# A linear-attention and token-mixing block: kv products by four token tiles, one low part behind `ol`, one high part on VectorE

## The chip, the core and the metric

The kernel runs on one NeuronCore of a Trainium2 chip. The metric is device time in microseconds for one execution, the median of the runs shown. The profile is one further execution with the hardware profiler on.

## What is computed

`x` is 2048 tokens by 512 channels. Two residual stages follow each other:

```
h  = x + A(layernorm(x))      # linear attention, 32 heads of 16
h2 = h + B(layernorm(h))      # MLP across the 2048 tokens, F = 1792

A: q, k, v = split(x @ wqkv);  pq = q @ w_phi (per head), pk = k @ w_phi
   phi = concat(softmax(p), softmax(-p))            # for q and for k
   kv  = sum over tokens of phi_k^T v;  z = sum over tokens of phi_k
   o   = (phi_q kv) / (phi_q z + 1e-6);  A = o @ wo
B: h = layernorm again; u = gelu(h^T @ w1 + b1); y = u @ w2 + b2, transposed back
```

All in float32. A large product is made as three products of a high part and a low part of each operand (`mm3`: high by high, high by low, low by high); a high part is a rounded copy and a low part is what the copy left.

## The kernel before

**Tiles.** Tokens go by 16 tiles of 128 (`NT`), called t below; channels by four blocks of 128.

**Prelude (lines 217 to 356).** `wqkv` arrives as twelve row blocks. Blocks 4 to 7 belong to k: each is centred (`center`), multiplied with the block-diagonal `w_phi` on TensorE (`fold`) and split into a high part (`hi_w`, ScalarE, or VectorE with `True`) and a low part (`lo_w`, VectorE). The order on TensorE, VectorE, ScalarE and GpSimd is written out by hand up to line 350. `proj(0, ..., True)` makes the first k product by parts: all high weights first (eight products), the low weights last (four).

**k/v stage (lines 358 to 415).** For each t: `k_logits` (TensorE product `pk_ps`, VectorE maximum, minimum and two subtractions, ScalarE exponential), `k_norm` (VectorE sums `sk`, GpSimd multiplies `pk`, and adds it to `zacc`), `v_proj` (TensorE `pv`, ScalarE scales into `vs`), and at six of the tiles the product, logits, exponential and sums of a q tile (`pu`, `eq`, `smq`). `v_kv` runs `kv` for the last two tiles after each second v: 16 products per tile, each with 32 columns of `vs` as weights and 64 columns of `pk`, all added up in one PSUM tile `kvp`. The order of this stage on each engine is made by a planner that simulates the program, so an edit here can move anything in the stage.

**From line 417 the order is by hand.** The last k and v products, then `zB` (line 484: `zacc` summed over tokens on TensorE), which GpSimd needs for every `s_ez` (`ez`, the products of phi_q with z); `s_den` sums `ez` on VectorE and makes the weights `w`, and `s_pq` multiplies `eq` by `w` on GpSimd.

**Attention loop (lines 660 to 701).** 18 iterations `it`; different tiles stand at different steps. In iteration `it`, TensorE does `pn` (phi_q kv of tile it-1, line 547), the transposes `tr` of tile it (line 529), a first piece of other work (half a q product, later a row block of w1), `po` (the product with `wo` of tile it-1, lines 62 to 64, twelve products) and then the rest of the other work (`turn`). On the other engines: ScalarE makes `oh` (high part of `pn`), copies `tr`, and before that takes the moments of the last h (`s_moments`); VectorE makes `ol` (low part of `pn`), sums `smq`, `s_den`, and `h` (the residual, line 572, which reads `po`); GpSimd makes `s_pq`, one reciprocal root, `s_ez` and the low part of `hs`. `pn` and `po` share one PSUM tile: `po` cannot start before `ol` has read `pn`, and the next `pn` cannot start before `h` has read `po`.

The row blocks of w1 come by DMA (`stream`): each has a high part on ScalarE (`his`) and a low part `wlo` on VectorE, made by `flush` at the end of each iteration:

```
    run(ql[:2] + ol + ql[2:] + sm if ql else sm[:1] + ol + sm[1:])
    ...
    if 0 <= it - 1 < NT:
        s_h(it - 1)
    flush()
```

**After the loop** come the rest of the first MLP product, gelu, and the second MLP product (`py`, line 795) with its own split of w2.

Of the kernel before, what the change touches and what calls it, by code (L numbers as in the profile page):

```python
# [9 lines left out]
F32 = mybir.dt.float32  # L10
# [7 lines left out]
P = 128  # L18
S, D, H, DH, F = 2048, 512, 32, 16, 1792
NT = S // P  # L20
KD = D // P
NF = F // P
NG = 8
NPR = 2 * NG
Q_AT = (4, 6, 8, 9, 11, 13)
V_NOT = (0, 1, 11)
Q_TURNS = ((0, 1), (0, 1), (0, 1), (0, 1), (0,), (1,), (0,), (1,))
LAG = 3
WARM = 9
# [4 lines left out]
def block_kernel(ctx: ExitStack, tc: tile.TileContext, x, xT, wT, phic, wo, w1, b1, w2, b2,  # L34
# [34 lines left out]
    wqp = aq.enter_context(tc.tile_pool(name="wqp", bufs=1, side="right"))  # L69
# [1 line left out]
    wql = wqp.tile([P, KD, D], F32R, name="wql")  # L71
    kvB = wqp.tile([P, 2, P], F32, name="kvB")
    kvS = wqp.tile([P, 4, 64], F32, name="kvS")
    sums = wqp.tile([P, NT, NPR, 2, 2], F32, name="smq")
    wqp.tile([P, 504], F32, name="pad")
    wk = aq.enter_context(tc.tile_pool(name="wk", bufs=4, side="right"))

# [7 lines left out]
    kk = a1.enter_context(tc.tile_pool(name="kk", bufs=2))  # L85
# [9 lines left out]
    X, XH, EQ, PK, VS, SQ, PS, W = {}, {}, {}, {}, {}, {}, {}, {}  # L95
# [10 lines left out]
    def split_x(t, raw):  # L106
        X[t] = big.tile([P, 2, KD, P], F32R, name="xs", tag="big")
        split(X[t][:, 0], X[t][:, 1], raw, nc.gpsimd)
# [25 lines left out]
    def signs(e):  # L134
        return e.rearrange("p g (a c h d) -> p (g a) c h d", a=2, c=2, h=2)
# [19 lines left out]
    def negate():  # L155

        if MN:
            ev, mx, mn = MN.pop(0)
            nc.gpsimd.tensor_sub(mn, mn, mx)
            nc.gpsimd.tensor_sub(ev[:, :, 1], mn.unsqueeze(3).to_broadcast([P, NPR, 2, DH]), ev[:, :, 0])  # L160

    def turns(*lists):

        return [ops[i] for i in range(max(map(len, lists))) for ops in lists if i < len(ops)]

    def run(*lists):
        for op in turns(*lists):
            op()

    def exps(t, e):  # L170
        nc.scalar.activation(e, e, AF.Exp, scale=r1[:, t:t + 1])
# [2 lines left out]
        return e.rearrange("p g (a d) -> p (g a) d", d=DH)  # L174

    def k_ops(t, o):
        PK[t] = kk.tile([P, NG, P], F32, name="pk", bufs=len(V_NOT) + 3)
        run(logit_ops(o, PK[t], False))

    def k_logits(t):  # L180
# [1 line left out]
        exps(t, PK[t])  # L182

    def v_out(t, o):
        VS[t] = kk.tile([P, D], F32, name="vs", bufs=4)
        nc.scalar.activation(VS[t], o, AF.Copy, scale=r1[:, t:t + 1])

    def v_proj(t):
        v_out(t, proj(t, wvh, wvl, ps_v, "pv"))
# [11 lines left out]
    def kv(t):  # L201

        for n in range(4):
            for c in range(4):
                g = n // 2 * 4 + c
                j = 2 * g + n % 2
                nc.tensor.matmul(kvp[32 * c:32 * c + 32, n, :], VS[t][:, 32 * j:32 * j + 32],  # L207
                                 PK[t][:, g, n % 2 * 64:n % 2 * 64 + 64], start=(t == 0 and n == 0),
                                 stop=(t == NT - 1), skip_group_check=True)

    def q_sum(t):

        SQ[t] = sums[:, t]
        e = signs(EQ[t])
        return [lambda c=c: nc.vector.reduce_sum(SQ[t][:, :, 1 - c], e[:, :, c], axis=AX.X) for c in range(2)]

    with tc.tile_pool(name="prep", bufs=1) as prep:
# [54 lines left out]
        def parts(c):  # L272
            return [w[:, :, c % 4 * P:(c % 4 + 1) * P] for w in HL[c // 4]]

        def hi_w(c, vector=False):
            if vector:
                nc.vector.tensor_copy(parts(c)[0], FO[c])
            else:
                nc.scalar.activation(parts(c)[0], FO[c], AF.Copy)

        def lo_w(c):
            hi, lo = parts(c)
            nc.vector.tensor_sub(lo, FO[c], hi)
# [4 lines left out]
        with tc.manual_schedule(engines={ET.PE, ET.DVE, ET.Activation, ET.Pool}):  # L288

            nc.gpsimd.tensor_mul(ph.rearrange("p c (a f) -> p c a f", f=DH),  # L290
                                 pc[:, 0:64].rearrange("p (c f) -> p c f", f=DH).unsqueeze(2).to_broadcast([P, 4, 8, DH]),
                                 pc[:, 64:72].unsqueeze(1).unsqueeze(3).to_broadcast([P, 4, 8, DH]))
            center(4, True)
            center(5, False)
            fold(4, ps_q, "pu")
            center(6, True)
            fold(5, ps_q, "pu")
            center(7, False)
            fold(6, ps_v, "pv")
            fold(7, ps_v, "pv")  # L300
            hi_w(4, True)
            hi_w(5, True)
            hi_w(6)
            split_x(0, xr[0])
            hi_w(7)
            for c in range(4, 8):
                lo_w(c)
            split_x(1, xr[1])
            k0 = proj(0, wkh, wkl, ps_k, "pk_ps", True)
            center(8, True)  # L310
            for c in range(9, 12):
                center(c, False)
            k1 = proj(1, wkh, wkl, ps_k, "pk_ps")
            for c in range(8, 12):
                fold(c, *((ps_q, "pu"), (ps_v, "pv"))[c // 10])
            k_ops(0, k0)
            split_x(2, xr[2])
            k_ops(1, k1)
            stats_x(0)
            k2 = proj(2, wkh, wkl, ps_k, "pk_ps")  # L320
            for c in range(8, 12):
                hi_w(c)
            for c in range(8, 12):
                lo_w(c)
            stats_x(1)
            exps(0, PK[0])
            split_x(3, xr[3])
            split_x(4, xr[4])
            v0 = proj(0, wvh, wvl, ps_v, "pv")
            k_ops(2, k2)  # L330
            stats_x(2)
            k3 = proj(3, wkh, wkl, ps_k, "pk_ps")
            k_norm(0)
            center(0, True)
            v_out(0, v0)
            exps(1, PK[1])
            center(1, False)
            exps(2, PK[2])
            v1 = proj(1, wvh, wvl, ps_v, "pv")
            k_ops(3, k3)  # L340
            fold(0, ps_q, "pu")
            fold(1, ps_q, "pu")
            k_norm(1)
            center(2, False)
            v_out(1, v1)
            hi_w(0)
            hi_w(1)
            lo_w(0)
            lo_w(1)
            center(3, False)  # L350
# [35 lines left out]
    def v_kv():  # L386

        nonlocal v
        v_proj(v)
        if v % 2 == 0:  # L390
            kv(v - 2)
            kv(v - 1)
        v += 1

    v = 2
    load_h(4)
    stats_x(4)
    for t in range(3, NT - 1):
# [3 lines left out]
        if t > 3:  # L402
            k_logits(t)
        if t > 3 and t not in V_NOT:
            v_kv()
# [93 lines left out]
    run(q_logits(0))  # L499
    assert v == NT  # L500
    q_mm()
    kv(NT - 2)
    kv(NT - 1)
    run(s_den(2, ps_d, "dn"))
    nc.vector.tensor_mul(kvS, kvp, mask.unsqueeze(1).to_broadcast([P, 4, 64]))

# [88 lines left out]
    COMING, LATER = [], []  # L595

    def his():
        while COMING:
            LATER.append(COMING.pop(0))
            _, raw, wh_ = LATER[-1]  # L600
            nc.scalar.activation(wh_, raw, AF.Copy)  # L601

    def flush():
        his()
        while LATER:
            wl_, raw, wh_ = LATER.pop(0)
            LO.append(nc.vector.tensor_sub(wl_, raw, wh_).ins)  # L607

# [40 lines left out]
    def turn(it):  # L649

        halves = Q_TURNS[it] if it < len(Q_TURNS) else ()
        n = [FN[0] <= it - LAG and FN[0] < NT, min(2, max(0, it - LAG + 1 - FN[1])) if q["logits"] == NT else 0]
        for p in range(2):
            ahead = n[p] + 1 + p + 2 * (it == NT)
            if it >= (LAG - 1, len(Q_TURNS) - 1)[p] and FL[p] < min(NT, FN[p] + ahead):
                fill_load(p)
# [3 lines left out]
    for it in range(NT + 2):  # L660
        if it < NT:
            s_x(it)
        shifted = q["logits"] - len(MN)
        ql = q_logits(0)
        work = turn(it)
        if it > NT:
            his()
        if 0 <= it - 2 < NT:
            s_moments(it - 2)
        if 0 <= it - 1 < NT:  # L670
            s_num(it - 1)
        if it < NT:
            s_tr(it)
        if it + 1 < NT:
            s_pq(it + 1)
        for w in work[:1]:
            w()
        if it == 0:
            s_kv()
        if q["exp"] < shifted:  # L680
            q_exp(0)
        if 0 <= it - 2 < NT:
            s_rstd(it - 2)
        if it + 3 < NT:
            s_ez(it + 3)
        if 0 <= it - 2 < NT:
            s_hn(it - 2)
        negate()
        his()
        sm = q_sums(0) if it == 0 or q["sum"] <= it + 2 else []  # L690
        ol = s_ol(it - 1) if 0 <= it - 1 < NT else []
        run(ql[:2] + ol + ql[2:] + sm if ql else sm[:1] + ol + sm[1:])
        if it > 0 and it + 2 < NT:
            run(s_den(it + 2, ps_t, "tr"))
        if 0 <= it - 1 < NT:
            s_wo(it - 1)
        for w in work[1:]:
            w()
        if 0 <= it - 1 < NT:
            s_h(it - 1)  # L700
        flush()
    flush()
    ms.close()
    a2.close()
# [101 lines left out]
    for n, (sp, p) in enumerate(STEPS):  # L806
        t = 2 * sp
# [93 lines left out]
```

## Time and profile before

| | us |
|---|---|
| median of 3 runs | 528.13 (528.08 to 528.7) |
| the profiled execution, whole | 528.31 |
| its span, first to last instruction | 526.5 |
| TensorE busy | 518.9 |
| VectorE busy | 386.2 |
| ScalarE busy | 278.2 |
| GpSimd busy | 229.1 |
| granted TensorE clock, mean | 0.998 |

A matmul's record overlaps the next one, so the distance between the starts of two records is what a product takes of TensorE's time, not the length of the record. In a row of a timeline stand the start in microseconds from the start of the span, the time, the engine, the line, the operation, output and inputs with their shapes, the count of records, and in brackets the idle time of the engine just before with what ended it. In a row of the chain stand the start, the time and the work. Each kv product and each small float32 product leaves two records.

### The profile page before, as it was taken

How to read it: one execution, taken by the hardware profiler on the slowest of the kernel's cores; microseconds unless marked ns; L12 is line 12 of the kernel's file. 1: busy time of each engine (PE TensorE's matmuls, PEld its weight loads, DVE VectorE, ACT ScalarE, POOL GpSimd, SP SyncE). 2: the span in 40 equal slices, each digit the busy share in tenths (PEclk: the TensorE clock that was granted, in tenths of full speed). 3: DMA queues.
4: the chain of work that ended last, by engine and by line, in shares of the span. 5: the costliest groups of instructions: out<-in, count | busy, mean ns of one | idle time of the engine just before them, and what ended most of it. 6: DMA issues, size and time to landing. Idle time of an engine off the chain costs nothing.

```text
span 526.5 us, 10155 instructions
## 1 busy us (share of the span) xinstructions
PE 518.9 (99%) x4000; PEld 446.6 (85%) x4000; DVE 386.2 (73%) x680; ACT 278.2 (53%) x476; POOL 229.1 (44%) x174
## 2 busy tenths in 40 slices
PE   8999999999999999999999999999999999999996
PEld 7788888887877777787788888888899999999996
DVE  6993999986897899887335425826668878887784
ACT  6998834525267878677657423526444243343330
POOL 2589699876999999884224000000001101101110
PEclk9999999999999999999999999999999999999999
DMA  8644210012303233333245433532015566535631
GB/s 307 203 122 120 83 40 21 1 40 103 99 25 101 101 97 109 114 103 122 81 142 178 119 91 92 169 112 81 20 41 112 146 144 151 128 123 121 161 67 54
DMA packets 45487, 55.85 MB, mean 106 GB/s; under 512 B 3968, under 2 KB 33024, under 8 KB 45440
## 3 DMA queue, kind: packets, MB, share of 16 engines
q1 hardware_dynamic: 43136, 51.38, 30.9%
q0 software_dynamic: 2016, 3.67, 5.3%
q8 instruction: 31, 0.51, 0.4%
q10 hardware_dynamic: 288, 0.17, 0.1%
q14 instruction: 16, 0.13, 0.1%
HBM read 46.81 MB, written 8.39 MB: 105 GB/s over the span
## 4 chain that ended last, share of the span: by engine, by line
PE 95%; DVE 3%; ACT 1%; issue 0%; DVEq 0%
PE py L795 26%; PE pu L62 13%; PE pu L63 12%; PE pu L64 12%; PE pv L63 3%; PE pv L64 3%; PE po L62 3%; PE pv L62 3%; PE po L64 3%; PE po L63 3%; PE pk_ps L62 2%; PE pk_ps L64 2%; PE pk_ps L63 2%; PE pn L547 2%; PE tr L529 2%; PE kvp L207 2%
## 5 line engine op out<-in xcount | busy, mean ns | idle before, releaser
L833 POOL DMA_DIRECT2D out<-ot x14 | 12.4, 998 | 211.4 <-DVE ot L831 211.4
L795 PE MATMUL py<-uf,whi 128*128 128x256 f32 x560 | 96.2, 283 | 0.0
L57 ACT ACTIVATE whi<-wraw 128x1792 fp32r<-128x1792 f32 x28 | 47.7, 1704 | 77.9 <-PE py L795 70.5
L62 PE MATMUL pu<-hs,whi 128*128 128x512 f32 x224 | 87.7, 394 | 0.0
L63 PE MATMUL pu<-hs,whi 128*128 128x512 f32 x224 | 87.2, 389 | 0.0
L64 PE MATMUL pu<-hs,wlo 128*128 128x512 f32 x224 | 86.7, 389 | 0.0
L795 PEld LDWEIGHTS py<-uf,whi 128*128 128x128 f32 x560 | 83.3, 192 | 0.0
L607 DVE TENSOR_TENSOR wlo<-wraw,whi 128x512 fp32r<-128x512 f32 x56 | 48.5, 872 | 44.6 <-ACT whi L601 44.4
L795 PE MATMUL py<-uf,wlo 128*128 128x256 f32 x280 | 69.9, 283 | 0.0
L58 DVE TENSOR_TENSOR wlo<-wraw,whi 128x1792 fp32r<-128x1792 f32 x28 | 56.6, 2022 | 16.7 <-ACT whi L57 16.6
L601 ACT ACTIVATE whi<-wraw 128x512 fp32r<-128x512 f32 x56 | 34.6, 625 | 45.0 <-PE pu L63 40.8
L62 PEld LDWEIGHTS pu<-hs,whi 128*128 128x128 f32 x224 | 42.0, 188 | 9.2 <-ACT hj L579 0.2
L795 PEld LDWEIGHTS py<-uf,wlo 128*128 128x128 f32 x280 | 49.7, 192 | 0.0
L64 PEld LDWEIGHTS pu<-hs,wlo 128*128 128x128 f32 x224 | 42.1, 188 | 8.9
L63 PEld LDWEIGHTS pu<-hs,whi 128*128 128x128 f32 x224 | 42.0, 188 | 8.3
L441 POOL TENSOR_TENSOR ez<-eq,zB 128x1024 f32<-128x1024 f32 x16 | 38.5, 2407 | 3.9 <-ACT zB L485 3.9
L795 PE MATMUL py<-un,whi 128*128 128x256 f32 x224 | 38.4, 283 | 0.0
L195 POOL TENSOR_TENSOR pk<-pk,sk 128x1024 f32<-128x1024 f32 x16 | 31.0, 1939 | 9.9 <-DVE sk L194 7.4
L795 PEld LDWEIGHTS py<-un,whi 128*128 128x128 f32 x224 | 33.2, 192 | 0.1
L465 POOL TENSOR_TENSOR eq<-eq,w 128x1024 f32<-128x1024 f32 x16 | 32.9, 2055 | 0.8 <-DVE w L462 0.8
L199 POOL TENSOR_TENSOR zacc<-zacc,pk 128x1024 f32<-128x1024 f32 x13 | 31.2, 2402 | 0.5
L58 POOL TENSOR_TENSOR hs<-hn,hs 128x512 fp32r<-128x512 f32 x16 | 20.7, 1293 | 17.9 <-ACT hs L57 17.9
(171 smaller groups left out, 1173.4 us busy)
## 6 DMA issues: line engine op xcount, KB each, us to landing
wraw<-in_w SPq DMA_DIRECT2D x112, 256.0 KB, 2.9
xraw<-in_xT SPq DMA_DIRECT2D x16, 256.0 KB, 3.0
xh<-in_x SPq DMA_DIRECT2D x16, 256.0 KB, 2.6
h<-in_x SPq DMA_DIRECT2D x16, 256.0 KB, 2.6
out<-h SPq DMA_DIRECT2D x16, 256.0 KB, 2.0
out<-ot POOLq DMA_DIRECT2D x14, 256.0 KB, 4.7
wraw<-in_wT SPq DMA_DIRECT2D x12, 256.0 KB, 5.2
wo<-in_wo SPq DMA_DIRECT2D x4, 256.0 KB, 4.0
```

The source lines that it names most:

```text
L57: nc.scalar.activation(hi, src, AF.Copy)
L58: lo_engine.tensor_sub(lo, src, hi)
L62: nc.tensor.matmul(o, ah, bh, start=first, stop=False)
L63: nc.tensor.matmul(o, ah, bl, start=False, stop=False)
L64: nc.tensor.matmul(o, al, bh, start=False, stop=last)
L195: nc.gpsimd.tensor_mul(heads(PK[t]), heads(PK[t]), sk.unsqueeze(2).to_broadcast([P, 2 * H, DH]))
L199: nc.gpsimd.tensor_add(zacc, zacc, PK[t])
L441: nc.gpsimd.tensor_mul(EZ[t], EQ[t], zB)
L465: nc.gpsimd.tensor_mul(heads(EQ[t]), heads(EQ[t]), W[t].rearrange("p g c h -> p (g c h)").unsqueeze(2).to_broadcast([P, 2 * H, DH]))
L601: nc.scalar.activation(wh_, raw, AF.Copy)
L607: LO.append(nc.vector.tensor_sub(wl_, raw, wh_).ins)
L795: nc.tensor.matmul(o, a[x], b[:, y], start=start and i == 0, stop=stop and i == 2, skip_group_check=True)
```

## The change

Three edits and the room that they need:

- `kv` is called for four tiles after each fourth v, not for two after each second. The tiles `pk` and `vs` have more buffers for it (8 for 6, and 5 for 4), and the q sums share 8 slots in place of 16.
- In the attention loop the last `flush` of an iteration makes at most one low part. One that is left over is made in the next iteration, behind `ol` and ahead of the sums.
- In the prelude the high part of k's third block (`hi_w(6)`) is made on VectorE in place of ScalarE.

```
+SUMS = 8
-    sums = wqp.tile([P, NT, NPR, 2, 2], F32, name="smq")
+    sums = wqp.tile([P, SUMS, NPR, 2, 2], F32, name="smq")
-        PK[t] = kk.tile([P, NG, P], F32, name="pk", bufs=len(V_NOT) + 3)
+        PK[t] = kk.tile([P, NG, P], F32, name="pk", bufs=len(V_NOT) + 5)
-        VS[t] = kk.tile([P, D], F32, name="vs", bufs=4)
+        VS[t] = kk.tile([P, D], F32, name="vs", bufs=5)
-        SQ[t] = sums[:, t]
+        SQ[t] = sums[:, t % SUMS]
...
-            hi_w(6)
+            hi_w(6, True)
...
-        if v % 2 == 0:
-            kv(v - 2)
-            kv(v - 1)
+        if v % 4 == 0:
+            for t in range(v - 4, v):
+                kv(t)
...
-    kv(NT - 2)
-    kv(NT - 1)
+    for t in range(NT - 4, NT):
+        kv(t)
...
-    def flush():
-        his()
-        while LATER:
+    def flush(n=None):
+        if n is None:
+            his()
+        for _ in range(len(LATER) if n is None else min(n, len(LATER))):
             wl_, raw, wh_ = LATER.pop(0)
             LO.append(nc.vector.tensor_sub(wl_, raw, wh_).ins)
...
+        left = len(LATER)
         his()
         sm = q_sums(0) if it == 0 or q["sum"] <= it + 2 else []
         ol = s_ol(it - 1) if 0 <= it - 1 < NT else []
-        run(ql[:2] + ol + ql[2:] + sm if ql else sm[:1] + ol + sm[1:])
+        run(ql[:2] + ol + ql[2:] if ql else sm[:1] + ol)
+        flush(left)
+        run(sm if ql else sm[1:])
...
-        flush()
+        flush(1)
```

In the built program the kv products stand in five blocks on TensorE where they stood in nine: of 1, 63, 64, 64 and 64 products, in place of 14 and 18 (a fold of four products between them) and seven times 32. In the attention loop one `wlo` moves in three places, from the end of iterations 8, 10 and 12 to behind `ol` of iterations 9, 11 and 13; nothing else in the loop changes its place. In the k/v stage the planner's order of k, v and q products differs from before on all engines.

## The prediction

> **What bounds the kernel now.** I read the chain that ended last first, then TensorE's own waits, then the timelines around each place that the change touches.
>
> ```profile
> PE 95%; DVE 3%; ACT 1%; issue 0%; DVEq 0%
> ```
> ```profile
> core 0 of [0], span 526.5 us
> PE pk_ps L287 <- DVE eps L53: 1.1, 1, 1.1
> PE po L62 <- DVE ol L556: 1.0, 1, 1.0
> PE pk_ps L124 <- ACT wkh L279: 0.8, 1, 0.8
> PE pn L547 <- DVE h L572: 0.2, 1, 0.2
> ```
>
> 95% of the chain is TensorE, and in 526.5 us TensorE waits four times for another engine, 3.1 us in all. So time is saved by work or switching taken off TensorE, or by one of these waits; the change is lost where it makes a new wait. Edit one is of the first kind, edit two aims at the 1.0 (ol), edit three at the 0.8 (wkh). About 0.2% (1.06 us) is what a measurement of this kernel can tell from no change.
>
> **Edit one: kv by four tiles.** It removes no product: 256 kv products stay. What goes is the passage into and out of a block. TensorE's timeline at one block:
>
> ```profile
> 85.33 0.39 PE L63 MATMUL pv<-wvl,xs 128*128 128x512 f32 x1
> 85.56 0.39 PE L64 MATMUL pv<-wvh,xs 128*128 128x512 f32 x1
> 85.88 1.10 PE L207 MATMUL kvp<-pk,vs 128*32 128x64 f32 x64
> 86.91 0.50 PE L62 MATMUL pk_ps<-wkh,xs 128*128 128x512 f32 x1
> 87.24 0.40 PE L63 MATMUL pk_ps<-wkl,xs 128*128 128x512 f32 x1
> ```
>
> Large products start every 0.23 (85.33, 85.56). Into the block the distance is 0.32, out of it 0.33 (86.91 to 87.24): 0.09 + 0.10 = 0.19 lost outside. Inside, the chain has blocks of three lengths:
>
> ```profile
> 36.45 0.57 PE kvp L207 x28
> ...
> 38.10 0.68 PE kvp L207 x36
> ...
> 53.52 1.03 PE kvp L207 x64
> ...
> 141.65 1.03 PE kvp L207 x64
> ```
>
> From 28 to 36 records 0.11, so 0.0138 a record; 64 records are 0.88 of the 1.03, and 0.15 is paid once per block. A block's passage is 0.19 + 0.15 = 0.34. The bounds are 0.19 (no fixed part) and 0.43: the 64 and 28 rows differ by 0.46 over 36 records, so 0.82 for 64 and 0.21 fixed, plus 0.19, rounded up. I take 0.34, the middle row pair being of like blocks. Before there are nine blocks (the two pieces, and seven of 64 records from 53.52 to 141.65); the order of the built program shows five after. Four fewer: 1.36, bounds 0.8 and 1.7.
>
> The Trainium skill (TensorEngine Tiling (Array Packing), Key Properties) says that a change of tiling mode drains the TensorE, and the skill's page TensorE: Matmul & The Clock Gate (Step-by-step) gives about 128 cycles of drain at 2.4 GHz, by which a block with two changes would cost some 0.11 us, an estimate from that page, and edit one 0.43 in all. The rows above show more than that, 0.19 outside the block alone, so the rows decide.
>
> Not all of it arrives. The fourth merge lies behind zB, and GpSimd and VectorE run the loop's head from zB:
>
> ```profile
> 124.72 2.19 DVE L476 TENSOR_TENSOR zacc<-zacc,pk 128x512 f32<-128x512 f32 x2 [0.41 <-POOL pk L195]
> 127.79 1.72 PE pk_ps L484 x4
> 130.22 2.40 POOL L441 TENSOR_TENSOR ez<-eq,zB 128x1024 f32<-128x1024 f32 x1 [3.86 <-ACT zB L485]
> 148.42 0.68 DVE L556 TENSOR_TENSOR ol<-pn,oh 128x512 fp32r<-128x512 f32 x1
> 149.19 0.46 PE L62 MATMUL po<-woh,oh 128*128 128x512 f32 x1
> 52.00:100.00 48.00, 48.00 (x389) 39.24 (x388) 47.75 (x80) 26.65 (x41) 42.81 (x29) 1.00 0.14 40
> ```
>
> The first ez waited 3.86 for zB, and the first po (149.19) started just when the first ol was done (148.42 + 0.68 = 149.1). VectorE works from zB to that ol without a gap, so this ol comes earlier by what zB gains: seven blocks stand before zB now, four after, 3 x 0.34 = 1.0. The last 0.34 becomes a wait at this po. **Term one: -1.0.**
>
> What could eat it: VectorE is busy 47.75 of 48 us from 52 to 100 (third number after the stretch's length, behind PE and PEld). In the new order the first q product, with which that stretch begins, stands behind more k and v work, and by the block prices its end is 0.4 later. TensorE did not once wait for VectorE there, and the k product of the last tile comes 1.9 earlier: ahead of it stood six blocks with ten token tiles, and now three with eight (3 x 0.34, and 64 records less, 0.88). The last zacc ended at 126.9 and was wanted at 127.79: 0.9 of room, against 1.0 needed and at least 1 gained on k's chain. A kv block of four also needs the fourth tile's `pk` from GpSimd and `vs` from ScalarE; blocks that stand 0.3 to 1.9 earlier find both long done. The new buffers keep the first k of a second round from waiting: eight `pk` are two blocks of four.
>
> **Edit two: the second low part behind ol.** It moves three subtractions of VectorE, no DMA, and passes no queue but VectorE's: behind it stand one sum, s_den and h, for which `w` (GpSimd) and the next pn (TensorE) wait. The first place, iterations 8 and 9:
>
> ```profile
> 204.11 1.19 DVE L607 TENSOR_TENSOR wlo<-wraw,whi 128x512 fp32r<-128x512 f32 x1
> 204.11 3.53 DVE L607 TENSOR_TENSOR wlo<-wraw,whi 128x512 fp32r<-128x512 f32 x2
> 207.57 0.67 DVE L215 TENSOR_REDUCE smq<-eq 128x32 f32<-128x512 f32 x1
> 208.16 0.68 DVE L556 TENSOR_TENSOR ol<-pn,oh 128x512 fp32r<-128x512 f32 x1
> 205.73 0.60 ACT L551 ACTIVATE oh<-pn 128x512 fp32r<-128x512 f32 x1
> 204.71 2.39 POOL L465 TENSOR_TENSOR eq<-eq,w 128x1024 f32<-128x1024 f32 x1
> 207.06 1.00 POOL L583 TENSOR_TENSOR r<-ve,mhalf 128x1 f32<-128x1 f32 x1
> 207.46 0.40 PE L64 MATMUL pu<-hs,wlo 128*128 128x512 f32 x1
> 208.90 0.50 PE L62 MATMUL po<-woh,oh 128*128 128x512 f32 x1 [1.04 <-DVE ol L556]
> ```
>
> po would have followed the product at 207.46 at 207.69; it started at 208.90, and restarting costs 0.1 more (0.33 for 0.23): 1.3 lost. The first wlo ends at 205.3, the second only at 207.6, when GpSimd's multiplication (204.71 to 207.10) has let it in. With the second behind ol, the sum runs at 205.3, ol waits for oh (206.33) and ends at 207.05, before po can start: the wait goes whole. **Term two: -1.3** (bounds: 0, were ol not earlier, and 1.3). The moved wlo then starts as that multiplication ends (207.10) and is done at 207.6; the second sum starts there, where it stood behind ol (208.16 + 0.6) before, so s_den and h are not late.
>
> The second place, iteration 11, is less kind:
>
> ```profile
> 224.53 0.68 DVE L556 TENSOR_TENSOR ol<-pn,oh 128x512 fp32r<-128x512 f32 x1
> 228.50 0.69 DVE L572 SCALAR_TENSOR_TENSOR h<-po,h 128x512 f32<-128x512 f32 x1 [0.16 <-PE po L64]
> 224.39 2.41 POOL L441 TENSOR_TENSOR ez<-eq,zB 128x1024 f32<-128x1024 f32 x1
> 231.12 0.67 PE L547 MATMUL pn<-pht,kvB 64*32 64x128 f32 x32
> ```
>
> Here the wait never was (no bracket on its po in the waits), and the moved wlo comes when ez has started. The rows show the two engines taking turns: r took 1.00 at 207.06 because a wlo ran in it. So wlo stands until ez ends (226.4 to 226.8), and all behind slides by 1.8: h from 228.50 to 230.3, done at 231.0, with pn at 231.12. It just fits; but ScalarE takes h's moments ahead of the next oh, so the next ol slides too. Cost 0 to 1.8; I take 0.3, since the room up to pn, 1.9, covers nearly all. At the third place GpSimd has no ez left to run. **Term three: +0.3.**
>
> The Trainium skill (SBUF — State Buffer, SBUF: two separate sides) calls the shared port pair of VectorE and GpSimd an exclusive lock, held for the whole instruction by whichever started first. It speaks against this edit, and the 1.00 row agrees; what it would do to all three places is the third rival.
>
> **Edit three: hi_w(6) on VectorE.**
>
> ```profile
> 9.53 0.59 ACT L279 ACTIVATE wkh<-pv 128x512 fp32r<-128x512 f32 x1
> 10.76 0.68 DVE L255 TENSOR_REDUCE mu<-wraw 128x1 f32<-128x512 f32 x1
> 12.13 1.09 PE L124 MATMUL pk_ps<-wkl,xs 128*128 128x512 f32 x4
> ```
>
> ScalarE's last high part starts at 9.53 and could start when its fold is done, about 0.1 earlier; the 0.8 wait is mostly that fold. VectorE gets one more copy (0.7) ahead of four low parts that ended at 10.8, now at 11.7; TensorE wants them at 12.13. The cover is 0.4; gone, the copy would cost up to 0.7. Bounds -0.8 and +0.7. **Term four: -0.1**, nearest to the fold.
>
> **The sum.** -1.0 - 1.3 + 0.3 - 0.1 = -2.1. The profiled execution took 528.31 (span 526.5 and 1.8 around it), so 526.2; the median of the runs is 0.18 lower, so 526.0. Its own range, by the bounds taken singly, is 525.4 to 526.6.
>
> **Rivals.** *The k/v gain does not come* (0.14): VectorE's full stretch starts 0.4 later, passes this on through the last zacc, and zB has TensorE wait. For it speaks 47.75 of 48; against it the 0.9 of room and the 1.9 by which k's last product comes sooner. Then 526.0 + 1.0 = 527.0, half of it within 0.2%.
>
> *All of it comes* (0.12): no wait at the first po, none in iteration 11, and the 0.2 at pn gone: -1.36 - 1.3 - 0.1 - 0.3 = -3.1, 525.0.
>
> *The lock turns edit two round* (0.08, slower): each moved wlo comes just after a GpSimd multiplication has started and is held 2.4 and takes 0.7. Then h is 3.1 late, 1.2 more than the 1.9 of room at pn, and ScalarE's moments behind h put 0.5 on the next po: 3 x 1.7 = 5.1 against the 2.4 gained: +2.7, 530.8. It decides where a wlo is held for more than 1.9 at all three places. Against it: at the first place the multiplication's end and the wlo's start fall within 0.1, and at the third no ez runs.
>
> *Edit two only exchanges its wait* (0.06): po(8) is on time and pn(9) waits as long: 526.0 + 1.3 = 527.3, no difference. That kv is not merged is ruled out by the order of the build; that only one of three moves meets a wait is in the sum.
>
> **The numbers.** My forecast has 0.60. Faster: 0.60 + 0.12 + 0.07 = 0.79. Within 0.2%: 0.07 + 0.06 = 0.13. Slower: 0.08. The range from 524.9 to 527.8 leaves out the slower case and the edge of the best one.
>
> **What would show it.** Right: five kvp blocks in the chain; zB's product near 126.7; a wait at the first po of 0.3 to 0.4; none at po(8); about 0.3 at pn or po of iterations 11 and 12. Wrong: TensorE waiting anywhere between 32 and 126, a wait for zacc at zB, h ending after pn is wanted in iterations 9 or 13, or kv blocks whose passage is not 0.34.

## The result and the profile after

| | before | after |
|---|---|---|
| median of six runs each, us | 528.39 (528.05 to 528.95) | 526.01 (525.63 to 526.15) |
| ratio, 95% interval | | 0.9953 [0.994, 0.9966] |
| profiled execution, whole / span | 528.31 / 526.5 | 526.04 / 524.3 |

The changed kernel is 2.4 us faster; 526.0 was forecast, as the likeliest of five cases.

First the chain of work that ended last, shares by engine, and TensorE's waits, both of the changed kernel. Line numbers are one to six higher than before.

```profile
PE 95%; DVE 3%; ACT 1%; issue 0%; DVEq 0%; ACTq 0%
```
```profile
core 0 of [0], span 524.3 us
PE pk_ps L289 <- DVE eps L54: 1.1, 1, 1.1
PE pk_ps L125 <- ACT wkh L281: 0.7, 1, 0.7
PE pn L549 <- DVE h L574: 0.2, 1, 0.2
```

The 1.0 for `ol` is gone and no row has come in its place. A wait of some tenths inside a row of products does not show in this list; it shows in the distances between starts. So the two traces are compared by five marks on TensorE. The rows of the marks, after, from TensorE's timeline:

```profile
10.18 2.11 PE L125 MATMUL pk_ps<-wkh,xs 128*128 128x512 f32 x8 [0.69 <-ACT wkh L281]
...
141.19 0.71 PE L531 MATMUL tr<-ident,eq 64*128 64x64 f32 x16
...
152.39 0.67 PE L549 MATMUL pn<-pht,kvB 64*32 64x128 f32 x32
...
203.89 0.67 PE L549 MATMUL pn<-pht,kvB 64*32 64x128 f32 x32
```

These are the first k product, the first transposes, and `pn` of tiles 1 and 8; `pn` of tile 9 started at 212.18, of tile 12 at 237.22. Before, the transposes and `pn` of tiles 8 and 9 were these:

```profile
142.61 0.71 PE L529 MATMUL tr<-ident,eq 64*128 64x64 f32 x16
...
204.96 0.67 PE L547 MATMUL pn<-pht,kvB 64*32 64x128 f32 x32
...
214.57 0.67 PE L547 MATMUL pn<-pht,kvB 64*32 64x128 f32 x32
```

The distances, in us, from the starts of the records:

| from, to | before | after | difference |
|---|---|---|---|
| first k product, first transposes | 132.44 | 131.01 | -1.43 |
| first transposes, pn(1) | 10.84 | 11.20 | +0.36 |
| pn(1), pn(8) | 51.50 | 51.50 | 0.00 |
| pn(8), pn(9) | 9.61 | 8.29 | -1.33 |
| pn(9), pn(12) | 24.81 | 25.04 | +0.23 |
| pn(12), last product | 282.42 | 282.39 | -0.03 |
| sum | 511.63 | 509.43 | -2.20 |

Four places moved, and each is one of the prediction's first three terms or a part of one. Edit three works ahead of the first mark and cannot show here; the first k product itself started at 10.17 and 10.18.

**The kv blocks.** The chain after the change, start, time and work (a first block of two records, at 49.26 in the timeline, is not on the chain), and TensorE's timeline around one block:

```profile
52.29 1.92 PE kvp L208 x126
84.35 1.92 PE kvp L208 x128
116.41 1.92 PE kvp L208 x128
126.73 1.72 PE pk_ps L486 x4
139.33 1.92 PE kvp L208 x128
```
```profile
83.96 0.39 PE L65 MATMUL pv<-wvh,xs 128*128 128x512 f32 x1
84.28 1.99 PE L208 MATMUL kvp<-pk,vs 128*32 128x64 f32 x128
86.20 0.50 PE L63 MATMUL pk_ps<-wkh,xs 128*128 128x512 f32 x1
86.54 0.40 PE L64 MATMUL pk_ps<-wkl,xs 128*128 128x512 f32 x1
```

Five blocks. The way in is 0.32 (83.96 to 84.28), the way out 0.34, as with 64 records; twice the records cost 1.92 where 64 cost 1.03, so 64 more cost 0.89 and the fixed 0.14 is paid once. zB's product (126.73 in the chain) stood at 127.79: 1.06 earlier.

**The first po.** VectorE's and TensorE's timelines after:

```profile
123.12 2.15 DVE L478 TENSOR_TENSOR zacc<-zacc,pk 128x512 f32<-128x512 f32 x2
...
146.75 0.68 DVE L153 TENSOR_REDUCE mn<-pu 128x32 f32<-128x512 f32 x1
147.35 0.68 DVE L558 TENSOR_TENSOR ol<-pn,oh 128x512 fp32r<-128x512 f32 x1
...
151.14 0.69 DVE L574 SCALAR_TENSOR_TENSOR h<-po,h 128x512 f32<-128x512 f32 x1
```
```profile
147.57 0.40 PE L65 MATMUL pu<-wqh,xs 128*128 128x512 f32 x1
148.09 0.50 PE L63 MATMUL po<-woh,oh 128*128 128x512 f32 x1
```

`ol` starts at 147.35 for 148.42, 1.07 earlier, no more than zB; `po` follows the product at 147.57 by 0.52 where 0.23 is usual. The transposes came 1.42 earlier, `po` 1.10.

**Iteration 9**, GpSimd, VectorE and TensorE:

```profile
203.63 2.38 POOL L467 TENSOR_TENSOR eq<-eq,w 128x1024 f32<-128x1024 f32 x1
```
```profile
205.29 0.69 DVE L558 TENSOR_TENSOR ol<-pn,oh 128x512 fp32r<-128x512 f32 x1 [0.48 <-ACT oh L553]
205.90 0.68 DVE L610 TENSOR_TENSOR wlo<-wraw,whi 128x512 fp32r<-128x512 f32 x1
```
```profile
206.39 0.39 PE L65 MATMUL pu<-hs,wlo 128*128 128x512 f32 x1
206.62 0.40 PE L63 MATMUL po<-woh,oh 128*128 128x512 f32 x1
```

`ol` now waits for `oh` and not for a low part, `po` follows by 0.23, and the moved `wlo` takes 0.68: GpSimd's multiplication ends at 206.01, as the `wlo` starts.

**Iterations 11 and 12**, the same engines:

```profile
221.55 2.41 POOL L443 TENSOR_TENSOR ez<-eq,zB 128x1024 f32<-128x1024 f32 x1
```
```profile
221.84 0.69 DVE L558 TENSOR_TENSOR ol<-pn,oh 128x512 fp32r<-128x512 f32 x1 [1.97 <-ACT oh L553]
222.45 2.06 DVE L610 TENSOR_TENSOR wlo<-wraw,whi 128x512 fp32r<-128x512 f32 x1
...
227.58 0.69 DVE L574 SCALAR_TENSOR_TENSOR h<-po,h 128x512 f32<-128x512 f32 x1
...
228.19 2.10 DVE L610 TENSOR_TENSOR wlo<-wraw,whi 128x512 fp32r<-128x512 f32 x1
230.21 0.67 DVE L217 TENSOR_REDUCE smq<-eq 128x32 f32<-128x512 f32 x1
230.80 0.68 DVE L558 TENSOR_TENSOR ol<-pn,oh 128x512 fp32r<-128x512 f32 x1
```
```profile
231.22 0.39 PE L65 MATMUL pu<-hs,wlo 128*128 128x512 f32 x1
231.54 0.50 PE L63 MATMUL po<-woh,oh 128*128 128x512 f32 x1
```

The moved `wlo` stands beside `ez` and lasts 2.06, until 0.5 after its end. `h` comes late for it, 2.10 of the next `wlo` and a sum follow without a gap, and `ol` ends at 231.48, while `po` would have followed the product at 231.22 by 0.23, at 231.45; it starts at 231.54 and takes 0.33 to its next.

### The profile page after: what moved, and what is told of

Same layout as the page of the kernel before. It is cut to its first block, busy times and chain, and to the rows that moved or that the text cites. A ratio compares the mean times of both kernels' runs of the same rounds, so it can differ in the third digit from the quotient of the medians.

```text
span 524.3 us, 10150 instructions
## 1 busy us (share of the span) xinstructions
PE 517.7 (99%) x4000; PEld 446.6 (85%) x4000; DVE 384.5 (73%) x681; ACT 277.8 (53%) x475; POOL 229.4 (44%) x174
## 4 chain that ended last, share of the span: by engine, by line
PE 95%; DVE 3%; ACT 1%; issue 0%; DVEq 0%; ACTq 0%
PE py L801 26%; PE pu L63 13%; PE pu L64 12%; PE pu L65 12%; PE pv L64 3%; PE pv L65 3%; PE po L63 3%; PE pv L63 3%; PE po L65 3%; PE po L64 3%; PE pk_ps L63 2%; PE pk_ps L65 2%; PE pk_ps L64 2%; PE pn L549 2%; PE tr L531 2%; PE kvp L208 2%
## 5 line engine op out<-in xcount | busy, mean ns | idle before, releaser
L610 DVE TENSOR_TENSOR wlo<-wraw,whi 128x512 fp32r<-128x512 f32 x56 | 47.3, 847 | 44.7 <-ACT whi L603 44.5
L172 ACT ACTIVATE pk<-pk,r 128x1024 f32<-128x1024 f32 x16 | 18.4, 1147 | 17.9 <-DVE pk L150 17.7
```

## The experiments

The median after each label is of the runs of that kernel; the ratio is to runs of the kernel before on the same chip. The distances are those of the table above, from the start of one profiled execution's first k product; they leave out what comes ahead of it, which differed between executions by up to 1.0 us (last section).

**Each edit alone.** Kernels made from the one before:

```
e1   kv by four tiles, with its buffers and SUMS; nothing else
e2   left = len(LATER) ... flush(left) ... flush(1); nothing else
e3   -            hi_w(6)
     +            hi_w(6, True)
```

> The kernel before with kv by four token tiles (and its buffers) alone. Theory of passages (0.34 us for each block of kv products): four blocks fewer than before, so TensorE reaches the first transposes 1.4 us sooner; the first po then waits 0.3 to 0.4 for ol, as VectorE and GpSimd start from zB, which has only three fewer blocks ahead of it. Time 1.0 to 1.1 us under before (ratio 0.998), and the wait of 1.0 us at po(8) stays. Rival, the order of the k/v stage (the planner's new order, not the passages, brought the time): the passages in the trace would still cost 0.34 each, but TensorE would gain something other than 4 x 0.34 between the first fold and the transposes, or all of 2.4 us.

> The kernel before with the second low part behind ol alone. Theory: the wait of 1.04 us at po(8) goes and 1.3 us with it; a new wait of 0.2 to 0.3 us stands at po(11), since the low part moved into iteration 11 waits out the ez multiplication on GpSimd. Time 1.0 to 1.1 us under before (ratio 0.998). Rival (the wait is only exchanged): po(8) on time but pn(9) or po(9) later by as much, ratio 1.000.

> The kernel before with hi_w(6) on VectorE alone. Theory: between 0 and -0.1 us, nothing that can be measured; TensorE's wait at the first k product shrinks by 0.1 at most since the fold of the last k block sets it. Rival (the copy starts the whole kernel sooner): -0.5 us or more. Rival (VectorE becomes late): k's low parts after 12.1 us, +0.3 us or more.

| | median, us | ratio, 95% | to transposes | to pn(1) | pn(8) to pn(9) | pn(9) to pn(12) | sum |
|---|---|---|---|---|---|---|---|
| before (profile) | 528.27 | | 132.44 | 10.84 | 9.61 | 24.81 | 511.63 |
| e1, kv by four | 527.32 | 0.9981 [0.9972, 0.999] | 131.09 | 11.21 | 9.58 | 24.81 | 510.59 |
| e2, low part behind | 527.37 | 0.9985 [0.9977, 0.9994] | 132.44 | 10.86 | 8.29 | 25.04 | 510.49 |
| e3, high part | 527.87 | 0.9993 [0.9984, 1.0002] | 132.43 | 10.84 | 9.59 | 24.81 | 511.51 |

Every place of the whole change has one edit as its cause: -1.35 and +0.37 come with kv alone, -1.33 and +0.23 with the low part alone. kv by four leaves the other wait where it was, as its list of TensorE's waits shows:

```profile
PE po L63 <- DVE ol L557: 1.0, 1, 1.0
```

The sums of e1 and e2, -1.04 and -1.14, make -2.18 for -2.20 in the whole, so these two edits neither help nor hinder each other. The high part works ahead of the first mark; the -0.12 of its sum is spread over several stretches by 0.04 or less, and the kernel with the buffers alone (below), where every instruction keeps its place, differs by 0.04. The high part's interval holds 1.

**One kv block for each tile.** The opposite of edit one, to price a block by adding blocks:

```
-        if v % 2 == 0:
-            kv(v - 2)
-            kv(v - 1)
+        for t in range(0 if v == 2 else v - 1, v):
+            kv(t)
...
-    kv(NT - 2)
     kv(NT - 1)
```

> The kernel before with kv called for one token tile after each v: 18 blocks of kv products stand in the build where there were 9, the products being the same. Theory of passages: nine blocks more at 0.34 us, 3.1 us over before (ratio 1.006), of which the part that stands ahead of zB also delays the loop. Rival (order of the k/v stage, or the buffers): no fixed relation to the number of blocks; if only the planner's order counted, within 1 us of before.

Measured: 531.4 us, ratio 1.0062 [1.0049, 1.0076], 18 blocks. Its chain shows blocks of half the records:

```profile
54.84 0.58 PE kvp L207 x32
63.81 0.58 PE kvp L207 x32
```

To the transposes it took 135.77, 3.33 more with nine blocks more: 0.37 each. Edit one saved 1.35 with four fewer: 0.34 each. The passage has one price in both directions, within 10%, though the planner orders the stage anew in each build, so the order is not needed to explain edit one's time.

**The two small losses.** From the changed kernel, on one chip:

```
e6   -  run(ql[:2] + ol + ql[2:] if ql else sm[:1] + ol)
     +  run((ol + ql if it == 1 else ql[:2] + ol + ql[2:]) if ql else sm[:1] + ol)
e7   -  flush(1)
     +  flush(2 if it == 10 else 1)
e8   both
```

> The changed kernel once more, beside the three below, for comparison with them: ratio to the kernel before 0.995 (-2.3 us), the first po again 0.4 late, the po of iteration 12 again 0.23 late. A theory by which the 2.3 us were a chance of one chip says 0.997 or more.

> The changed kernel, but in iteration 1 VectorE takes ol ahead of the two reductions over q (mx, mn) that stand before it. My theory: the first po waits 0.42 only because VectorE comes to ol late; with ol 1.2 us earlier it starts on time, the stretch of TensorE between the first transposes and the next falls from 6.09 to 5.67, and the kernel is 0.4 us faster than the changed one. Rival: the wait only goes to a place behind (q's PSUM tile is free 0.6 later, so a q product or the sums for the next pn wait): stretch shorter by 0.4, next stretch longer by about as much, time as the changed kernel's.

> The changed kernel, but in iteration 10 both low parts are taken at the iteration's end, as before the change, so that none stands behind ol in iteration 11, where ez holds it. My theory: the 0.23 that the po of iteration 12 loses goes, and nothing else changes: 0.2 us faster than the changed kernel, 7.02 for that stretch instead of 7.26. Rival: the 0.23 is the distance from pn back to large products and has nothing to do with the low part: the stretch stays at 7.26.

> Both edits of the two runs before together: if both theories hold, 0.6 us faster than the changed kernel, about 525.4 where that is 526.0, ratio to the kernel before 0.994; if the waits only move, as the changed kernel.

| | median, us | ratio, 95% | to pn(1) | pn(1) to pn(8) | pn(9) to pn(12) | sum |
|---|---|---|---|---|---|---|
| e5, as changed | 525.95 | 0.9961 [0.9946, 0.9976] | 11.20 | 51.52 | 25.00 | 509.43 |
| e6, `ol` first | 526.15 | 0.9959 [0.9947, 0.9971] | 11.20 | 51.75 | 25.02 | 509.70 |
| e7, two at ten | 525.61 | 0.9951 [0.9939, 0.9963] | 11.20 | 51.45 | 24.81 | 509.14 |
| e8, both | 525.92 | 0.9952 [0.9939, 0.9965] | 11.19 | 51.76 | 24.81 | 509.42 |

The medians of these four lie within 0.6 us and their intervals overlap; the distances tell more. The gain of the change came again on this chip (525.95). One of its six runs took 528.63, so the ratio is pulled up and its interval reaches 0.9976; but the distances sum to 509.43, as in the first profile of this kernel, and by that the gain is no chance of one chip.

`ol` first gained nothing. VectorE and TensorE of e6:

```profile
146.36 0.69 DVE L558 TENSOR_TENSOR ol<-pn,oh 128x512 fp32r<-128x512 f32 x1 [0.31 <-ACT oh L553]
146.97 0.68 DVE L152 TENSOR_REDUCE mx<-pu 128x32 f32<-128x512 f32 x1
...
151.35 0.69 DVE L574 SCALAR_TENSOR_TENSOR h<-po,h 128x512 f32<-128x512 f32 x1
```
```profile
147.62 0.40 PE L63 MATMUL po<-woh,oh 128*128 128x512 f32 x1
...
152.20 0.67 PE L549 MATMUL pn<-pht,kvB 64*32 64x128 f32 x32 [0.32 <-DVE h L574]
```

The first `po` is on time, with a record of 0.40 and no restart, and the same time is lost at the next `pn`, which waits for `h`: 11.20 to pn(1), as in the changed kernel. So the wait moved, as the rival said, but not because VectorE had to do all the same work ahead of `h` without a gap. With `ol` first VectorE stands 0.31 idle for `oh`, and `h` starts 10.35 after the first transposes (151.35 less 141.00) where it started 9.95 after them in the changed kernel (151.14 less 141.19). The idle time is most of that 0.40. An order with one reduction, then `ol`, then the other would have filled it, by these rows; it was not tried. From pn(1) to pn(8) 0.23 more is lost, and its cause stays open.

Taking both low parts in iteration 10 does what was expected. VectorE and TensorE of e7:

```profile
226.53 1.85 DVE L610 TENSOR_TENSOR wlo<-wraw,whi 128x512 fp32r<-128x512 f32 x1
228.31 0.67 DVE L217 TENSOR_REDUCE smq<-eq 128x32 f32<-128x512 f32 x1
229.93 0.69 DVE L558 TENSOR_TENSOR ol<-pn,oh 128x512 fp32r<-128x512 f32 x1 [0.95 <-ACT oh L553]
```
```profile
231.03 0.39 PE L65 MATMUL pu<-hs,wlo 128*128 128x512 f32 x1
231.25 0.39 PE L63 MATMUL po<-woh,oh 128*128 128x512 f32 x1
```

`ol` waits for `oh` again, and `po` follows by 0.22. The stretch pn(9) to pn(12) is back at 24.81, in e8 too. By this mark e7 beats both kernels, by 0.2 to 0.3 us against the changed one; the medians (525.61 for 525.95) agree but would not show it alone. Both edits together do not bring the 0.6 that was expected: e8's sum is the changed kernel's, since what the low part gains is lost between pn(1) and pn(8), as in e6.

**Less work for VectorE.** e6 left open whether VectorE's load holds the head of the loop. Of this edit one line is shown; `short` is set for iteration 1 alone:

```
...
-  nc.vector.tensor_reduce(mn, v, axis=AX.X, op=ALU.min)
+  nc.vector.tensor_reduce(mn, v[..., :4] if short else v, axis=AX.X, op=ALU.min)
...
```

> The changed kernel, but the minimum over q that VectorE takes in iteration 1, ahead of the first ol, is taken over 4 of 16 elements of each head; the other 12 are left out for that one tile. Order and all else stay. What the run with ol ahead showed (po on time, the next pn late by as much) can be read in two ways. My theory now: from zB on VectorE has no gap until h of iteration 1, so what counts is the work it has, not the order; with some 0.45 us less of it both ol and h come earlier, the first po starts on time (its stretch 5.7 instead of 6.09), no wait follows at pn, and the time falls by 0.35 to 0.4 against the changed kernel. Rival: pn's wait has another cause than VectorE's load: the stretch gets shorter and the next one longer again, no gain.

Measured: 525.57 us, ratio 0.9947 [0.9933, 0.996]. VectorE:

```profile
147.22 0.28 DVE L153 TENSOR_REDUCE mn<-pu 128x32 f32<-128x128 f32 x1
147.42 0.68 DVE L558 TENSOR_TENSOR ol<-pn,oh 128x512 fp32r<-128x512 f32 x1
```

0.40 less of VectorE's time gave 10.84 to pn(1), the kernel before's figure, and no later loss: pn(1) to pn(8) is 51.50, the sum 509.07. So the work that VectorE has ahead of `ol` holds the first `po`. That its order does not count, as the expectation has it, is not shown: e6 put the order round and by that made VectorE wait, and no run tried an order without such a wait. This kernel leaves out work and is no version to use.

**The buffers alone.**

```
+SUMS = 8;  pk bufs + 2;  vs bufs + 1;  sums[:, t % SUMS]
```

> The kernel before with the buffers alone of the change (two more pk, one more vs, eight places for q's sums); every engine's instructions stand in the order of the kernel before. Ratio to it 1.000; its distance from 1 shows how much a ratio of this kernel can be off where nothing is changed, against 0.9993 for the high part on VectorE alone. Theory: that 0.9993 is no more than chance, so a ratio as far from 1 can come here too. Rival: a gain of 0.1 is real and this ratio is nearer to 1.000.

Measured: 528.38 us, ratio 0.9999 [0.9991, 1.0008], sum 511.59. The room costs nothing. The interval is 0.0009 wide to each side, so e3's 0.9993 lies as far from 1 as chance may bring it; that the ratio here came out at 0.9999 speaks mildly for the rival, and settles nothing.

## Why the prediction was right, step by step

**Term one, -1.0.** Measured at pn(1): -1.07 in the whole (-1.43 and +0.36), -0.98 with e1 alone (-1.35 and +0.37). All three of its numbers held: the 0.34 of a passage (0.34 and 0.37), the part that passes zB (1.06 for 1.0), and the rest that becomes a wait at the first `po` (0.36 for 0.3 to 0.4). The reason given for it, that VectorE has no gap up to `ol`, is borne out by e9, where 0.40 less of its work put the first `po` on time. The stretch without a gap begins only with the first sum over `ez`, at 131.59 in the changed kernel; ahead of it VectorE stands 3.91 idle for the first `ez`, which needs zB. The estimate of 0.43 in all by the Trainium skill (TensorEngine Tiling (Array Packing), Key Properties, with TensorE: Matmul & The Clock Gate, Step-by-step) is ruled out by the 1.35: the drain that the pages name may be a part of the passage, and what the rest is no run here shows.

The danger named there did not come. VectorE's stretch is as full as before, with the busy time third behind the length:

```profile
52.00:100.00 48.00, 48.00 (x449) 39.80 (x448) 47.68 (x79) 27.41 (x42) 41.76 (x28) 1.00 0.14 40
```

but the last `zacc` ends at 125.27 and zB's product starts at 126.57 in the timeline. The room is 1.3. The prediction's 0.9 took zB's start from the chain; by the timeline, where it started at 127.63, the room before was 0.7. The first rival, 527.0, is out.

**Term two, -1.3.** Measured -1.33, in the whole and in e2. The `wlo` met the end of GpSimd's multiplication within 0.1, as worked out, so s_den and `h` were not late, and the rival that the wait is only exchanged (527.3) is out: `pn` of tile 9 came the whole 1.33 earlier.

**Term three, +0.3.** Measured +0.23, at the place named, iteration 12, and gone with e7. The path is a little different. `h` was late by 1.5 (227.58 for 226.11, which is 228.50 less the 2.39 by which everything came earlier), not 1.8, and it fitted under `pn`. But what made the next `ol` late was VectorE's own queue, not ScalarE: `oh` was ready at 230.17 (229.59 and 0.58, ScalarE's timeline), and `ol` stood behind a `wlo` of 2.10 and a sum until 230.80. ScalarE's moments were named as the cause; the rows do not bear that out. The 0.3 was also chosen from 0 to 1.8 and not summed, so that its size came out is in part luck.

The slower rival, the lock at all three places (530.8), needed a hold of more than 1.9 three times. It came nowhere: the moved `wlo` took 0.68, 2.06 and, in iteration 13, 0.68, so the one that was held was held for about 1.4. The Trainium skill (SBUF — State Buffer, SBUF: two separate sides) says that the port pair which VectorE and GpSimd share is an exclusive lock, held for the whole instruction by whichever started first. The 2.06 agrees: the `wlo` ended at 224.51, 0.55 after `ez` (223.96), which is about what a `wlo` takes by itself (0.60 from its start to the next in iteration 9). Whether the hold costs time was decided by what GpSimd does at that moment, which the timeline of before showed.

**Term four, -0.1.** The wait for `wkh` was 0.80 and is 0.69, the low parts end at 11.72 where 11.7 was worked out, and the last four low products stood at 12.13 as before. In the seven profiles with edit three the wait is 0.69; without it, 0.80 in three, but 0.73 in e4 and 0.69 in e1. The sign is likely and the size fits; with a ratio of 0.9993 [0.9984, 1.0002] it isn't shown.

**The sum** of -2.1 stands against -2.27 between the profiled executions and -2.38 between the medians; of the -2.27, -2.20 lies between the first k product and the last product. That 526.01 hits the forecast of 526.0 is in part luck: the kernel before had a median of 528.39 beside it and not 528.13, and the gain was larger by as much. The prediction's own range of 525.4 to 526.6 does not follow from the bounds that it names: term two at 0 would alone give 527.3, and term three at 1.8 alone 527.5.

## What to carry to other kernels

Price the change between two kinds of products from blocks of different length in the trace you have: the part that does not grow with the number of records, with the gaps on both sides, is what merging saves. Then follow the gain to the next engine that works without a gap: it arrives only up to there. Taking work off that engine let the rest through here; a new order of its work that made it wait for another engine did not. When a step is moved on one of two engines that hold each other up, look in the timeline at what the other one runs at the new place, for each iteration, since the same edit cost nothing in two places here and two tenths in the third.

## What the runs showed of the hardware that was not expected

The start of the program moves between executions without any edit there: the first k product stood at 10.17 in the kernel before and at 10.60 in the kernel with the buffers alone, and between 9.68 (e3) and 10.71 (e5) in all. From there on the two agree to 0.04 us over 511. VectorE's wait for the first weights' DMA was 2.51 in the one and 2.67 in the other, so the weights' arrival is a part of it; what makes the rest is not shown. In kv by four TensorE itself waits for weights that VectorE has still to centre:

```profile
PE pu L268 <- DVE wraw L258: 0.6, 1, 0.6
```

Half a microsecond is the size of the smaller effects here, so distances from a mark behind the loading told what the whole times could not.
